# Induced attention with a gated feed-forward layer: loads and big transposes in turn, shared blocks moved, row sets a block earlier

## The chip, the cores and the metric

The kernel runs on one core of one Trainium2 chip. The metric is the device time of one execution in microseconds (us). Besides single times there is one profiled execution, which gives the start and the duration of every instruction, and for each DMA the time at which it landed.

## The reference

Input: `x` of 4 batches x 12416 tokens x 128 channels, 32 inducing rows of 128 channels, and the weights of a gated layer (gate and value 128 x 1536, out 1536 x 128). Cut to what matters:

```python
def mab(q, kv):                          # softmax attention, scale 1/sqrt(128)
    s = scale * (q @ kv.transpose(0, 2, 1))
    a = exp(s - s.max(-1)); a /= a.sum(-1) + 1e-9
    return a @ kv
h   = mab(I, x)                          # 32 rows look at all tokens of a batch
y   = mab(x, h)                          # every token looks at the 32 rows
out = (sigmoid(y @ w_gate) * (y @ w_val)) @ w_out
```

## The kernel before, in words

**Two stages per batch.** In the first stage the 32 inducing rows attend to all tokens of a batch and give `h` (32 x 128). In the second stage every token attends to the 32 rows of `h`. Since the softmax weights of a token are only 32 numbers, `h` is multiplied into the weights once per batch (`hw`, `hw_mm`), and the gated layer then reads the 32 weights of a token (`rep`) in place of its 128 channels.

**Blocks.** The second stage goes over 97 blocks of 512 tokens: 24 a batch (three row sets `d` of two quads `i` of four blocks `r`) and one mixed block of the tails. A block has 12 feature slices `j`. For every pair of slices TensorE makes the gate (`g`) and ScalarE the tanh (`T`, `g_tanh`, L482). For each of the four chunks of a block TensorE fills the value of two slices (`va`) and of one slice (`vb`), and VectorE multiplies both with `T` (`v_mul`, L495). TensorE then multiplies the products `u` with `w_out` into `acc` (L538). ScalarE copies `acc` out (`oT`), SyncE transposes it by DMA (`on`, L562) and GpSimd issues the store (L566).

**Shared blocks.** In the blocks that `SHARED` names (the number within the batch), the first chunk is not VectorE's. Two extra slots among the gate slots fill its value, ScalarE copies it from PSUM to SBUF (`v`, L833), and GpSimd makes the product in two operations a slice (`v_mul_pool`, L508 and L511): two slices for the first extra slot, one for the second. Such a block has three chunks on VectorE.

**Row sets.** For each row set of eight blocks, `rep_events` (L691) lays a chain: job `s2` on TensorE with the exponential on ScalarE; `e2_dma`, a transpose; `s2_sum`, five additions on GpSimd that halve each time; `s2_rec`, a reciprocal on VectorE; `a2_mul`, two multiplications on GpSimd; `a2_dma`, two transposes; `rep_put`, two writes to a DRAM buffer `dt`; `rep_get`, two times four reads from it into `rep`. All DMAs of the chain are SyncE's.

**The next batch's first stage** runs beside the second stage of this one. Six quads of 2048 tokens are loaded by GpSimd with a cast (`load_x`, L125), transposed by one big DMA each (`xT_dma`, L192), scored two quads at a time (job `s1`, then `a1_dma`, L217), and summed into `h` (job `h`, `h_mm` L243, with `h_add` on VectorE, L267). `hfin` and `hw` end the batch.

**What sets the order.** Every engine's instructions stand in the order of the program; there is no scheduler. The string `PLAN` (L23) has one word for each block: `A` and `B` are the chunk's two value fills with their products, `G` is the next gate slot (`W` the same in a padded form), `J` the next extra job, and a letter from `a` to `l` the output matmul of that slice. Gate slots run about one and two thirds blocks ahead, since ten `T` buffers exist. DMAs and GpSimd's steps are tied to places: `at(n, k, f)` puts `f` ahead of chunk `k` of block `n` (written n.k below), and `put(n, k, ...)` queues a job in that order, which the next `J` takes. A place says only after which instructions of its engine a step stands. An engine with nothing to wait for runs ahead of the place; one that waits holds up all that stands behind it in its own queue.

```python
for q, ((ln, lk), (hn, hk)) in enumerate(zip(loads, hs)):
    at(n0 + ln, lk, load_x, nb, q)
    at(n0 + ln + 1, 2, xT_dma, nb, q)
    put(n0 + hn, hk, "h", nb, q)
```

Of the kernel before, what the change touches and what calls it, by code (L numbers as in the profile page):

```python
# [10 lines left out]
F16 = mybir.dt.float16  # L11
# [11 lines left out]


PLAN = (
    "GAGBWGAabGBcGAfeGBdGAhBWgJ AGilkjBGGAabcBGAfGBedGAhGgBiG AlkjBGGAbacBGAfWBedGAhJBgG "
    "AilkjBGGAabcBGAfWBedGAhGgBiG AlkjBGGAbaBcWAGfeBGdAGBhGg AGilkBjGAJBabcAGefBGdAGhgBGi "
    "AGlBkjJAGBaGbAGcGBefGAdhGBgG AikljBGGAbBaefGAdGBchG AgGBikGAljBJAGaBGbcGAGfBedG "
    "AhGgBiGAlJBkGAjJBGAGbacBfeG AGdhBgiAGlkjBGGAbBJaAGcfBGe AGdhBGgAGiBkljGAGBabef "
    "AGdBJcGAhgBGikAGljJBGAGbaBcfG AGedBGgAGhBilGAGkjBJAGBaGbcG AefGBdGAhgGBiGAkljBJAGbaGBcf "  # L30
    "AGeGdBhGAgiWBlGAkjJBG AGabfBecGAGdBghGAikGBlJjAGBaGbcG AfGBedGAhJBgGAilkjBGGAabBcefG "
    "AdGBghGAilkjBGGAbaBGcGAfBJe AGdhBGgAGilBkjGAGBabef AGdcBGgGAhiBkljGAGBbacfAGedgGBhG "
    "AilkjBGGAbacBWAGfBedGAhGgBiG AlkjBGGAbacBJAGfBGeAGdghBG AGilBkjGAGBbafeAGdcGBG "
    "AghBGiAGklBJjAGGBbacfAGedBGg AGhiBGkAGljBJAGBGabcGAeGfBdG AgGhBiGAlGkBjGAJbaBcAGfeBGdh "
    "AGgiGBkGAljBJAGbGBGa AGBefdGAGchBgGAiGBlkjGAGBabce AGfBJdAGhgBWiAGkBljGAGBbacf "
    "AGedGBghAGilkjBGGAabBGcAGefBGd AGhgBGiAGlkjBJGABbGafG AedGBcGAhgBWiGAklBjJGAaGbBcG "
    "AfeGBdGAhJBgGAilkjBGGAbacBfe AGdgGBhGAilkjBGGAaBJbAGceBGf AGdhBGgAGilkBjGAGBabef "
    "AGdcGBgGAhiBGkAGljBJAGBGbaceG AGfBdghGAiWBklGAjJBGAGabcBfG AGedBhGAgGBGAGilkJjBGAaGbBGcf "
    "AGedBWhAGgilBkjGAJaBbG AceGBfGAdhBWgGAilBkjGAJbBaG AcfGBeGAdBWghAGilkBjGGAabBceG "
    "AfGdBgGAhiBGGAlkjBGGAbacGBe AGfdBhGAGgilBkjAGGBbafe AGcdBGhAGgiBlkjGAGBabceAGfdBgG "  # L40
    "AGhikBljGAGBabcGAefBGdAGhgBGi AGlBkjGAGaBbcGAJBfeGAdGBhgG AilkjBGGAabfBedGAcGBhgG "
    "AikljBJGAbGBacGAfWBedAGhgGBiG AlkGBGAjBJAGbBGacGAfGBedG AhGgBiGAlGkBjGAGBbacfAGeBJd "
    "AGghBGiAGlkjBJGABbaGfG AedBchGGAgiBkljGAGBabceGAfBdGgh AGikljBGAJBbaGAcWBfeGAdGhBgG "
    "AilkjBGAGabBcGAeGBGAGfdBGh AGgikBGAGlBjJAGBbGae AGfdBGhGAgciBGAGlkBjJGABbGacG "
    "AfGeBdGAhgWBiGAkljBJAGbacBfG AeGBdGAhJBgGAilkjBGGAbacBfGG AedBghiGAlkjBGGAbaBfedG "
    "AGhBgciAGlkBjJGAaBbGcfAGedWBhgG AiGlBkGAjJBGAGabBcWAGfBedG AGhgBiGAlGkBjJAGBbaGGcAGfBJe "
    "AGdBGhgGAilkBjGAGbBafeG AdcGBgGAhiGBkGAljBJGAbacBfG AeGBdhGAgGiBlGAkjBWGAabBcefG "
    "AdGBghGAilkjBGGAbacBfeGAGBdGh AGgilBkjGAGBefbaAGdgBWh AGicBkljGAGBbacGAefdBGAGghBiG "
    "AGlkjBGAGBbacGAfeBWdAGhgBGi AGlBkjGAGBabcGAefGBdGAhGBgiG AkljBGGAfeBbadGAhWBgcG "
    "AilkBjGGAabBcGAfeGBdGAhgBGiG AlkBjGGAbaBcAGfWBedGAhgGBiG AlkjBJAGbacBGAfGeBGAdWBhgG "  # L50
    "AikljBGGAfedBabGAGhBgiG AclkjBGGAabcBGAGfBedGAhWgBiG AGlkBjGAGBbacAGefBWAGdhgBG "
    "AGiBlkjGAGBabcAGefBdJAGGhBgG AikGlBjGAGBabfeAGdgBWh AGciBkljGAGBabcGAefBGdAGhgiBG "
    "AGkljBGAGBbacGAfeBWdGAhgBGi AGlBkjGAGBabcGAefGBdGAJBhgG AilkjBGGAfeBbadGAGhgBcG "
    "AilBkjGGAabBcGAfBGedGAhgWiBG AlkjBGGAbacBGAGfeBdGAGBhgiG AlkjBGGAabcBGAGfeBdGAGBGhg "
    "AGiBlkjGAGBefabAGdhBWgG AicBlkjGAGBbacGAefBGdAGhgBGi AGlkBjGAGBbacGAefBWdGAhgBGi "
    "AGlBkjGAGBbacGAefGBdGAhGgBiG AlkjBGGAfebBadGAgWBhcG AikBljGGAabBcGAfeGBdGAhGBgiG "
    "AlkBjGGAbBacAGfBWedAGhgBGiG AlkBjGAGbaBcGAefBGdGAhGgBiG AlkjBGGAbafBeGAdWBhgG "
    "AcikBljGABaGbAcfeBdAhgBilkj"
)
SHARED = (3, 7, 11, 15, 19, 23)  # L60


@with_exitstack
def kernel(
# [9 lines left out]
    nc = tc.nc  # L74
# [26 lines left out]
    smp = ctx.enter_context(tc.tile_pool(name="smp", bufs=2))  # L101
# [308 lines left out]
    NBK = len(blocks)  # L410
# [274 lines left out]
    def at(n, k, fn, *a):  # L685
        ev.setdefault((n, k), []).append(lambda: fn(*a))

    def put(n, k, *a):
        extra.append((n, k, a))

    def rep_events(n, b, d):  # L691
        put(n, 1, "s2", b, d)
        at(n + 1, 0, e2_dma, b, d)
        at(n + 1, 3, s2_sum, b, d)
        at(n + 2, 3, s2_rec, b, d)
        at(n + 2, 3, a2_mul, b, d, 0)
        at(n + 2, 3, a2_mul, b, d, 1)
        at(n + 3, 0, a2_dma, b, d, 0)
        at(n + 3, 1, a2_dma, b, d, 1)
        at(n + 3, 2, rep_put, b, d, 0)  # L700
        at(n + 3, 3, rep_put, b, d, 1)
        at(n + 4, 0, rep_get, b, d, 0)
        at(n + 4, 1, rep_get, b, d, 1)

    def m_mul():
        e2s["m", "a2"] = s2n_mul("m", 0, nc.gpsimd, B)
# [20 lines left out]
    assert ND == 3  # L727
    for b in range(B):
        n0 = b * BB
        rep_events(n0 + 2, b, 1)  # L730
        rep_events(n0 + 10, b, 2)
        nb = b + 1
        if nb < B:
            if b == 0:
                loads = ((1, 0), (2, 0), (5, 0), (6, 0), (8, 0), (9, 0))
                s1s, s1t, fin = (5, 9, 12), 6, 16
                hs = ((8, 1), (9, 1), (12, 2), (13, 1), (14, 3), (15, 1))
            else:
                loads = ((-10, 0), (-7, 0), (-4, 0), (-1, 0), (2, 0), (5, 0))
                s1s, s1t, fin = (-2, 5, 9), 0, 14  # L740
                hs = ((1, 1), (3, 1), (7, 1), (8, 1), (12, 1), (13, 1))
            for q, ((ln, lk), (hn, hk)) in enumerate(zip(loads, hs)):
                at(n0 + ln, lk, load_x, nb, q)
                at(n0 + ln + 1, 2, xT_dma, nb, q)
                put(n0 + hn, hk, "h", nb, q)
            at(n0 + loads[1][0], 1, load_tail, nb)
            at(n0 + loads[1][0] + 1, 3, xTt_dma, nb)
            for e, sn in enumerate(s1s):
                put(n0 + sn, 1, "s1", nb, [2 * e, 2 * e + 1])
                at(n0 + sn + 1, 1, a1_dma, nb, [2 * e, 2 * e + 1])  # L750
            put(n0 + s1t, 1, "s1t", nb)
            put(n0 + fin, 1, "hfin", nb)
            put(n0 + fin + 1, 1, "hw", nb)
            at(n0 + fin + 2, 1, hw_pad, nb)
            rep_events(n0 + fin + 2, nb, 0)
        else:
            put(n0 + 6, 1, "s2m")
            at(n0 + 7, 1, s2n_sum, "m", 0, B)
            at(n0 + 7, 1, m_mul)
            at(n0 + 8, 1, m_dma)  # L760
# [76 lines left out]
    def out_one(n, j):  # L837
        out_mm(n, j, us.pop((n, j)))
        if done_out[n] == NJ:
            out_store(n)  # L840
        if stores and (done_out[n] == 10 or n >= NBK - 2):
            stores.popleft()()

    words = PLAN.split()
# [63 lines left out]
```

The softmax here doesn't subtract the row's maximum and nothing guards it: scores larger than these inputs give would overflow.

## Time and profile before

| | us |
|---|---|
| median of 8 runs | 709.43 |
| lowest, highest | 704.78, 711.69 |
| the profiled execution: its time | 707.12 |
| its span, first to last instruction | 705.3 |
| VectorE / ScalarE / TensorE busy in it | 666.3 / 662.5 / 678.9 |
| GpSimd busy in it | 309.5 |

How to read it: the span is 1.8 us shorter than the execution's own time, which has the start and the end in it too. The profile's page gives the busy time of each engine, a row of tenths over 40 slices of the span, and the costliest groups of instructions with their mean duration in ns and the idle time ahead of them. PE is TensorE, DVE VectorE, ACT ScalarE, POOL GpSimd, SP SyncE; PEld are TensorE's weight loads. SyncE has no busy time: its lines (SPq) show how long the issue of a DMA stood in its queue. A group "u<-T,va" writes `u` from `T` and `va`; buffer numbers are left out. L is the line in the kernel. Until about 29 us the first batch's own first stage runs by itself; then block 0 begins. Block 96 ends at about 700 us.

### The profile page before, as it was taken

The numbers are of one execution on the slowest core, as the hardware profiler recorded it, in microseconds if no ns is written. First come the engines' busy times: TensorE is split into PE (matmuls) and PEld (weight loads), VectorE is DVE, ScalarE is ACT, GpSimd is POOL, SyncE is SP. The second block draws the span as 40 slices with busy tenths as digits, with TensorE's granted clock in tenths as the row PEclk, the third lists the DMA queues.
The fourth block names the chain that finished last, engine by engine and source line by source line (L and its number), as shares of the span: only waits on it lengthen the run. The fifth ranks groups of instructions, "written<-read, shape, count | busy, mean of one in ns | idle before, by whom it ended". The sixth has DMA issues, their size and how long they took to land.

```text
span 705.3 us, 13070 instructions
## 1 busy us (share of the span) xinstructions
PE 678.9 (96%) x4561; PEld 238.4 (34%) x4561; DVE 666.3 (94%) x792; ACT 662.5 (94%) x773; POOL 309.5 (44%) x389
## 2 busy tenths in 40 slices
PE   8899899999999999999999989999999999999997
PEld 5433233333333333333333323333333333333334
DVE  2599899999999999999999989999999999999997
ACT  4699899999999989999999989999999999999995
POOL 5234506426536334365353540744632633633523
PEclk9999999999999999999999999999999999999999
DMA  9687999875898673676786792354282353362223
GB/s 176 99 130 131 192 164 174 171 138 100 169 175 135 124 153 75 128 156 111 162 163 110 132 204 60 84 136 82 60 143 68 68 150 75 68 150 69 65 49 76
DMA packets 163955, 85.95 MB, mean 122 GB/s; under 512 B 133392, under 2 KB 148144, under 8 KB 163888
## 3 DMA queue, kind: packets, MB, share of 16 engines
q1 hardware_dynamic: 143904, 45.95, 36.6%
q0 software_dynamic: 19696, 39.03, 26.5%
q8 instruction: 35, 0.57, 0.3%
q14 instruction: 32, 0.26, 0.1%
q10 hardware_dynamic: 288, 0.13, 0.1%
HBM read 39.34 MB, written 28.31 MB: 96 GB/s over the span
## 4 chain that ended last, share of the span: by engine, by line
PE 69%; ACT 10%; DVE 9%; DMA 5%; issue 3%; POOL 2%; SPq 1%; DVEq 0%; ACTq 0%; POOLq 0%
PE acc L538 30%; PE g L428 16%; PE vb L428 9%; DVE u L495 9%; PE va L428 8%; ACT T L482 6%; DMA a2T<-a 2%; ACT v L833 1%; DMA a1n<-e 1%; PE warm L190 1%; ACT oT L560 1%; PE h L255 1%; PE s L324 1%; PE x L428 1%; DMA rep<-dt 1%
## 5 line engine op out<-in xcount | busy, mean ns | idle before, releaser
L482 ACT ACTIVATE T<-g 128x1024 f16<-128x1024 f32 x582 | 559.6, 1038 | 17.2 <-PE va L428 7.8
L495 DVE SCALAR_TENSOR_TENSOR u<-T,va 128x1024 f16<-128x1024 f16 x365 | 444.8, 1219 | 5.8 <-PE va L428 2.8
L538 PE MATMUL acc<-u,wo 128*128 128x512 f16 x1083 | 340.8, 383 | 0.6
L495 DVE SCALAR_TENSOR_TENSOR u<-T,vb 128x512 f16<-128x512 f16 x365 | 248.7, 681 | 2.3 <-PE vb L428 1.8
L428 PE MATMUL g<-rep,hw 32*128 32x512 f16 x1086 | 205.3, 384 | 4.2 <-DMA rep<-dt 1.7
L428 PEld LDWEIGHTS <-hw 32*128 32x128 f16 x1854 | 77.4, 91 | 221.0 <-issue 207.9
L428 PE MATMUL va<-rep,hw 32*128 32x512 f16 x722 | 141.2, 380 | 4.5 <-DVE u L495 2.3
L566 POOL DMA_DIRECT2D out_dram<-on x96 | 53.8, 561 | 204.4 <-DMA on<-oT 185.1
L538 PEld LDWEIGHTS <-wo 128*128 128x128 f16 x1152 | 93.9, 97 | 146.1 <-issue 92.1
L428 PE MATMUL vb<-rep,hwp 128*128 128x512 f16 x361 | 137.9, 382 | 1.5 <-DVE u L495 0.7
L508 POOL TENSOR_TENSOR vt<-v,T 128x512 f32<-128x512 f32 x69 | 79.8, 1156 | 116.6 <-ACT v L833 72.5
L511 POOL TENSOR_TENSOR x<-vt,v 128x512 f16<-128x512 f32 x69 | 87.4, 1266 | 5.4
L428 PEld LDWEIGHTS <-hwp 128*128 128x128 f16 x450 | 43.8, 97 | 58.5 <-issue 26.4
L560 ACT ACTIVATE oT<-acc 128x512 f16<-128x512 f32 x96 | 59.1, 615 | 2.4 <-PE acc L538 1.8
L833 ACT COPY v<-x 128x1024 f32<-128x1024 f32 (+1 forms) x46 | 37.9, 824 | 0.7 <-PE x L428 0.6
L370 POOL TENSOR_TENSOR a<-e2n,rc 128x512 f16<-128x512 f16 x22 | 22.5, 1039 | 21.8 <-DVE rc L361 21.7
L538 PE MATMUL acc<-x,wo 128*128 128x512 f16 x69 | 24.1, 387 | 0.9 <-POOL x L511 0.7
L428 PE MATMUL g<-rep,hwp 128*128 128x512 f16 x66 | 19.6, 379 | 0.6 <-ACT T L482 0.6
L353 POOL TENSOR_TENSOR tree<-tree 128x256 f32<-128x256 f32 (+2 forms) x33 | 16.1, 489 | 2.6
L353 POOL TENSOR_TENSOR tree<-e2n 128x512 f32<-128x512 f16 x11 | 12.6, 1149 | 10.4 <-DMA e2n<-e 10.2
L127 POOL DMA_DIRECT2D xq<-in_x_dram x23 | 13.0, 566 | 0.8 <-POOLq L892 0.8
L584 DVE COPY xT<-xt 128x1024 f16<-128x1024 f16 x6 | 4.2, 692 | 9.6 <-PE xt L579 9.6
(98 smaller groups left out, 211.6 us busy)
## 6 DMA issues: line engine op xcount, KB each, us to landing
out_dram<-on POOLq DMA_DIRECT2D x96, 256.0 KB, 3.0
xq<-in_x_dram POOLq DMA_DIRECT2D x23, 512.0 KB, 6.9
rep<-dt SPq DMA_DIRECT2D x88, 128.0 KB, 2.9
dt<-a2T SPq DMA_DIRECT2D x22, 128.0 KB, 2.3
on<-oT SPq DMA_TRANSPOSE x96, 2.5
xq<-in_x_dram POOLq DMA_DIRECT2D x2, 256.0 KB, 14.5
wg<-in_moe_w_gate_dram POOLq DMA_DIRECT2D x1, 384.0 KB, 15.9
wv<-in_moe_w_val_dram POOLq DMA_DIRECT2D x1, 384.0 KB, 16.7
```

Source lines behind the costliest of these rows:

```text
L127: nc.gpsimd.dma_start(t[:], x[b, ds(q * QT, QT)].rearrange("(p j) c -> p (j c)", j=QT // P))
L353: nc.gpsimd.tensor_tensor(out=nxt, in0=cur[:, :, 0:w], in1=cur[:, :, w:2 * w], op=ALU.add)
L370: nc.gpsimd.tensor_tensor(out=a2[:], in0=e2n[:, i], in1=rc[:, i].unsqueeze(3).to_broadcast((P, 4, 4, M)), op=ALU.mult,)
L428: nc.tensor.matmul(ps[:, ds(col, TOK)], weights(k["b"]), rep[rows, 4 * k["i"] + k["r"]], start=True, stop=True,)
L482: nc.scalar.activation(out=Ts[(bi, p)][:, :, 0:T], in_=ps[:].rearrange("p (a t) -> p a t", a=2)[:, :, 0:T], func=AF.Tanh, scale=0.5,)
L495: nc.vector.scalar_tensor_tensor(out=u[:, :, 0:T], in0=Ts[(bi, j0 // 2)][:, j0 % 2:j0 % 2 + n, 0:T], scalar=1.0, in1=ps[:].rearrange("p (a ...
L508: nc.gpsimd.tensor_tensor(out=t[:], in0=v, in1=Ts[(bi, j0 // 2)][:, j0 % 2 + jj, :], op=ALU.mult)
L511: nc.gpsimd.tensor_tensor(out=u[:, jj, :], in0=t[:], in1=v, op=ALU.add)
L538: nc.tensor.matmul(accs[bi][:, 0:T], wo16[:, j, :], u, start=(c == 0), stop=(c == NJ - 1))
L560: nc.scalar.activation(out=oT[:], in_=accs[bi][:], func=AF.Copy, scale=0.5)
L566: nc.gpsimd.dma_start(out[ds(row0, QT)].rearrange("(p j) c -> p j c", j=QT // P)[:, 4 * k["r"]:4 * k["r"] + 4, :], on[:],)
L833: nc.scalar.copy(out=v32[:], in_=ps[:, 0:p * TOK])
```

## The change

It moves work and adds one kind of instruction; what is computed stays.

1. *First batch's loads.* The six quads of batch 1 are loaded every two blocks, at 0.2, 2.2, 4.2, 6.2, 8.2 and 10.2 (before: 1.0, 2.0, 5.0, 6.0, 8.0, 9.0), and each big transpose is placed four chunks after its load (before six; the later batches keep six).
2. *Fence.* Ahead of every load but a batch's first, GpSimd copies two elements a row out of the previous quad's transposed tile. So it waits for that transpose to land before it issues the load.
3. *Shared blocks* are those numbered 1, 5, 9, 13, 17, 21 in place of 3, 7, 11, 15, 19, 23. There are 23 in both kernels.
4. *Row sets* begin one block earlier within a batch (and the first set of batch 1 too), the sum stands a quarter of a block later after its start, the reciprocal and the multiplications three quarters of a block later; the two transposes, the two writes and the two groups of reads stand together at one place each.
5. *h jobs and scores* of the next batch are placed anew; in the later batches the third and fourth h stand at 8.1 and 8.3 in place of 7.1 and 8.1. In batch 0 the finish is one block earlier.
6. *Stores.* A block's store is issued when the block after the next has four of its output matmuls, in place of when the next block has ten.
7. `PLAN` is new for all this (its words are left out here). It has the same number of each letter except that five gate slots lose the padded form.

```diff
-SHARED = (3, 7, 11, 15, 19, 23)
+SHARED = (1, 5, 9, 13, 17, 21)
...
+    def load_fence(b, q):
+        t = smp.tile([P, 2], F16, tag="fence", name=f"fence_{b}_{q}")
+        nc.gpsimd.tensor_copy(out=t[:], in_=xTs[b][:, ds(q * QT, 2)])
...
     def rep_events(n, b, d):
         put(n, 1, "s2", b, d)
         at(n + 1, 0, e2_dma, b, d)
-        at(n + 1, 3, s2_sum, b, d)
-        at(n + 2, 3, s2_rec, b, d)
-        at(n + 2, 3, a2_mul, b, d, 0)
-        at(n + 2, 3, a2_mul, b, d, 1)
-        at(n + 3, 0, a2_dma, b, d, 0)
-        at(n + 3, 1, a2_dma, b, d, 1)
-        at(n + 3, 2, rep_put, b, d, 0)
-        at(n + 3, 3, rep_put, b, d, 1)
-        at(n + 4, 0, rep_get, b, d, 0)
-        at(n + 4, 1, rep_get, b, d, 1)
+        at(n + 2, 0, s2_sum, b, d)
+        at(n + 3, 2, s2_rec, b, d)
+        for i in range(2):
+            at(n + 3, 2, a2_mul, b, d, i)
+            at(n + 3, 3, a2_dma, b, d, i)
+            at(n + 4, 1, rep_put, b, d, i)
+            at(n + 4, 3, rep_get, b, d, i)
...
-        rep_events(n0 + 2, b, 1)
-        rep_events(n0 + 10, b, 2)
+        rep_events(n0 + 1, b, 1)
+        rep_events(n0 + 9, b, 2)
...
-                loads = ((1, 0), (2, 0), (5, 0), (6, 0), (8, 0), (9, 0))
-                s1s, s1t, fin = (5, 9, 12), 6, 16
-                hs = ((8, 1), (9, 1), (12, 2), (13, 1), (14, 3), (15, 1))
+                loads = ((0, 2), (2, 2), (4, 2), (6, 2), (8, 2), (10, 2))
+                s1s, s1t, fin = ((5, 0), (9, 2), (12, 3)), 6, 15
+                hs = ((8, 1), (8, 3), (13, 0), (13, 2), (14, 2), (15, 0))
+                wait = 4
             else:
                 loads = ((-10, 0), (-7, 0), (-4, 0), (-1, 0), (2, 0), (5, 0))
-                s1s, s1t, fin = (-2, 5, 9), 0, 14
-                hs = ((1, 1), (3, 1), (7, 1), (8, 1), (12, 1), (13, 1))
+                s1s, s1t, fin = ((-2, 1), (5, 1), (9, 1)), 0, 14
+                hs = ((1, 1), (3, 1), (8, 1), (8, 3), (12, 1), (13, 1))
+                wait = 6
             for q, ((ln, lk), (hn, hk)) in enumerate(zip(loads, hs)):
+                if q:
+                    at(n0 + ln, lk, load_fence, nb, q - 1)
                 at(n0 + ln, lk, load_x, nb, q)
-                at(n0 + ln + 1, 2, xT_dma, nb, q)
+                at(n0 + ln + (lk + wait) // 4, (lk + wait) % 4, xT_dma, nb, q)
                 put(n0 + hn, hk, "h", nb, q)
             at(n0 + loads[1][0], 1, load_tail, nb)
-            at(n0 + loads[1][0] + 1, 3, xTt_dma, nb)
-            for e, sn in enumerate(s1s):
-                put(n0 + sn, 1, "s1", nb, [2 * e, 2 * e + 1])
-                at(n0 + sn + 1, 1, a1_dma, nb, [2 * e, 2 * e + 1])
+            at(n0 + loads[1][0] + 2, 1, xTt_dma, nb)
+            for e, (sn, sk) in enumerate(s1s):
+                put(n0 + sn, sk, "s1", nb, [2 * e, 2 * e + 1])
+                at(n0 + sn + 1, 0, a1_dma, nb, [2 * e, 2 * e + 1])
...
-        if stores and (done_out[n] == 10 or n >= NBK - 2):
+        while stores and (n >= NBK - 2 or len(stores) > 1 and done_out[n] == 4):
             stores.popleft()()
```

## The prediction

> **What bounds the kernel now.** I read the page's first part, then the busy time of every engine by stretches, then the queues of SyncE (SP) and GpSimd (POOL) around the stretches that fall short. The first part names three engines as full:
>
> ```profile
> PE 678.9 (96%) x4561; PEld 238.4 (34%) x4561; DVE 666.3 (94%) x792; ACT 662.5 (94%) x773; POOL 309.5 (44%) x389
> L495 DVE SCALAR_TENSOR_TENSOR u<-T,va 128x1024 f16<-128x1024 f16 x365 | 444.8, 1219 | 5.8 <-PE va L428 2.8
> L495 DVE SCALAR_TENSOR_TENSOR u<-T,vb 128x512 f16<-128x512 f16 x365 | 248.7, 681 | 2.3 <-PE vb L428 1.8
> ```
>
> The two VectorE products of one chunk start 1.77 us apart from the next pair (they overlap by some 65 ns a piece), so an ordinary block of four chunks takes 7.05 us and a shared block of three 5.31 us. Read from the starts of the products, most blocks take just that, plus 0.41 for each h sum and 0.33 for each reciprocal. VectorE is the metronome; TensorE and ScalarE have a little air. The stretches show where the metronome stops (after a stretch's length come the busy times of PE, PEld, DVE, ACT and POOL):
>
> ```profile
> core 0: us, PE busy (x) PEld busy (x) DVE busy (x) ACT busy (x) POOL busy (x), PEclk, DMA share, GB/s
> 75.00:108.00 33.00, 30.19 (x202) 9.93 (x201) 28.97 (x35) 28.30 (x34) 10.82 (x13) 0.95 1.14 173
> 108.00:225.00 117.00, 115.97 (x772) 38.97 (x770) 116.53 (x139) 115.77 (x136) 59.64 (x73) 1.00 0.85 150
> 225.00:257.00 32.00, 30.05 (x206) 10.02 (x204) 30.02 (x37) 30.00 (x36) 15.80 (x20) 1.00 0.85 162
> 257.00:400.00 143.00, 140.83 (x913) 47.78 (x910) 142.31 (x169) 140.92 (x165) 66.07 (x83) 1.00 0.65 128
> 400.00:425.00 25.00, 22.14 (x138) 6.90 (x136) 21.10 (x26) 21.30 (x26) 11.20 (x13) 0.93 0.84 164
> 425.00:700.00 275.00, 270.47 (x1683) 94.91 (x1682) 274.38 (x320) 267.34 (x310) 117.06 (x136) 1.00 0.40 89
> ```
>
> Idle VectorE: 4.03 us in 75:108, 1.98 in 225:257, 3.90 in 400:425, together 9.9; in the other 535 us shown 1.8. So the most that any reordering can win is near 12 us, and 9.9 of it sits in three places. The first place, by the queue of SyncE and then VectorE:
>
> ```profile
> 66.62 1.20 SPq L384 DMA_TRANSPOSE a2T<-a  x1
> 69.20 2.20 SPq L562 DMA_TRANSPOSE on<-oT  x1
> 71.49 1.22 SPq L384 DMA_TRANSPOSE a2T<-a  x1
> 72.81 7.02 SPq L390 DMA_DIRECT2D dt<-a2T  x2
> 79.92 1.82 SPq L397 DMA_DIRECT2D rep<-dt  x4
> ...
> 83.81 1.22 DVE L495 SCALAR_TENSOR_TENSOR u<-T,va 128x1024 f16<-128x1024 f16 x1 [2.39 <-PE va L428]
> 85.98 0.69 DVE L495 SCALAR_TENSOR_TENSOR u<-T,vb 128x512 f16<-128x512 f16 x1 [0.94 <-PE vb L428]
> ```
>
> Two loads went out at 67.56 and 68.67. The second a2T was issued at 71.49 and landed at 79.49; the second dt, which reads it, stood at the head of SP's queue until then (7.02 us for two), and the rep reads behind it came late for block 8's first gate matmul. The other two places are one story: a row set's a2T transposes meet a load, SP stands, and behind them the a1n transpose is late for an h matmul:
>
> ```profile
> 414.62 2.01 SPq L397 DMA_DIRECT2D rep<-dt  x4
> 416.67 1.23 SPq L221 DMA_TRANSPOSE a1n<-e  x1
> ...
> 420.36 0.61 PE L245 MATMUL h<-a1n,ones 128*128 128x128 f16 x4 [2.64 <-DMA a1n<-e]
> ...
> 421.56 0.42 DVE L271 TENSOR_TENSOR hacc<-hacc,h 128x256 f32<-128x256 f32 x1 [2.95 <-PE h L255]
> ```
>
> **What the Trainium skill says.** "DMA: Bandwidth & Descriptors", section "Issuing engines are not separate DMA queues": DMAs of all engines share the same 16 DMA engines and interleave. The trace agrees that they share, but it is harsher than interleaving: over the 18 loads after 38 us, DMAs issued inside a load landed mostly 0.2 to 4 us after that load's own end, however small; a2T issued 0.9 us or more ahead of a load took 2.4 to 3.8 us, 0.3 to 0.7 us ahead 4.7 to 7.4. "TensorE: Matmul & The Clock Gate", section "What's actually happening": an idle PE falls to half clock and needs a few us of work to return. The trace agrees: after the two long waits matmuls show 0.61 instead of 0.39 us, and the granted clock is 0.93 to 0.95. "GPSIMD Engine Reference", "1. Specifications": GpSimd shares SBUF interfaces with VectorE, in contention for VectorE instructions with two SBUF inputs. The product reads one input from PSUM, and it took 1.16 to 1.22 us throughout, GpSimd busy or not: moving GpSimd work costs VectorE nothing.
>
> **The change part by part.** The totals of VectorE, ScalarE and TensorE work stay (23 shared blocks, 49 extra jobs, 365 pairs); five gate pairs lose the padded form. So only waits change. Positions (block.chunk) are turned into time with 1.765 us a chunk.
>
> *h a block later (8.1 and 8.3 for 7.1 and 8.1), row sets a block earlier.* From a1n's issue at 6.0 to h there are now over two blocks (15 us) for one (7 us). SP stood 4 to 7 us in the bad cases, so both waits for a1n go: -1.98 and -3.90. Likewise the old wait in 75:108 goes as it was, -4.03. Removed: 9.9.
>
> *What is late next, first batch.* The reciprocal and both a2_mul are at 4.2, 63.5 us. But the instruction order on GpSimd puts the first pair of shared block 5 ahead of a2_mul. Its gate slot is in chunk 4.0 (59.9); such v copies started 0.2 to 1.5 us after their chunk and take 1.03, so 62.2; 2 x (1.15 + 1.27) and gaps make 5.1: 67.3. A store 0.6, two a2_mul 2.1: 70.0. The fence and load q2 follow at 70.1; the second a2T leaves SP at 69.0 + 1.2 = 70.2, level with the load, so it lands near the load's end, 77. Then on SP: dt 0.4, an output transpose 1.2, and, which is new, the big transpose xT of q2 before the rep reads (1.3 to 3.2 us with no load in flight, 2.4 taken): 81.0; the first half of rep lands 2.7 later, 83.7. VectorE runs out at 38.4 + 6.98 + 14.1 + 7.38 + 5.31 + 7.05 + 1.77 = 81.0 (block 5 is the short one now) and restarts 1.2 after rep, as before: idle 3.9, and 1.1 of slow matmuls after it (1.64 before). Taken 5.0; bounds 2.0 (load and xT at their shortest) and 7.5 (both at the long end).
>
> *Batch 1, rows of blocks 8 to 15.* Same order: a2_mul ends 7.4 us after chunk 28.2, the load leaves at 10.7, so the a2T are free of it, but the rep reads (from 11) fall inside it and land near 17.5 to 18.5. The gate matmul that needs them comes at about 17.1. Taken 1.0 (0 to 2). The rows for blocks 40 on meet the next batch's first load in the same way: 1.0 (0 to 2).
>
> *Batch 2, rows of blocks 56 on.* Both pairs of block 53 stand ahead of a2_mul: it ends 8.5 us after chunk 52.2, the load leaves at 9.3, the second a2T 0.6 before it: lands at 13.5, the dt inside the load at 16.2, rep at 18.9, wanted at 16.8. Idle 2.1 and slow clock 0.9: taken 3.0 (0.5 to 4.5).
>
> *First batch, end.* a2_mul behind the pair of block 13, rep for block 16 due at 15.1 within 1 us of its landing, h of q4 at 14.2 within 1.5 us of a1n: 0.7 (0 to 3). In the other row sets without loads the chain from reciprocal to rep is 15 us against 17 to 23 available: 0.3.
>
> *Fence, stores, two jobs in shared blocks.* 15 fences, two elements each; the nearest row, a 32x128 copy, takes 0.29: 4 us of GpSimd in all, hidden in its 56% idle time, if the xT has landed; I find it landed 3 us or more before in every batch after the first. If that cover goes, the load and the stores behind it slip, and nothing due within 3 us. Stores go out half a block later, when their transpose (2.4 to 9.9 us) has landed: GpSimd's 185 us of waiting for it shrinks, worth nothing off the path. Six shared blocks carry two jobs; VectorE has 5.3 us there and TensorE nearly as much: 0.5 (0 to 2).
>
> Sum: -9.9 + 5.0 + 1.0 + 1.0 + 3.0 + 0.7 + 0.3 + 0.5 = +1.6. The profiled execution took 707.1 (span 705.3), so 708.7; the median of the eight runs is 709.4, 2.3 above it, so 711.0.
>
> **Rivals.** (a) The queues do clear: v copies come early in their slots, xT takes 1.8, loads 6.0. Then the first batch returns 2.5, batch 2 only 0.5, the rest 1. Net -5.9: 703.5. For it: the long waits of before came from two loads issued 1.1 us apart, and this pairing is gone. Against: a2_mul demonstrably moves behind 5 us of other GpSimd work. (b) Slower, by one mechanism: GpSimd's line. Each us that a shared pair ends later moves a2_mul, a2T and then the load onto each other; where a2T falls behind the load, rep slips by the whole load, some 4 us more than I took, once in each of batches 0, 1 and 2 (and the idle PE then runs slow): returns 20 in place of 11.5, net +9.5, 719. It decides when a v copy is over 1 us later than taken. (c) The products of shared blocks come late for their output matmuls (0.7 us waited in all before): pairs have 7 to 12 us from slot to use, as before, so 0 to 2 us; within the likeliest case.
>
> **How the numbers follow.** Likeliest, stalls change place: 0.45, 707.5 to 714.5. (a) 0.24. (b) 0.29. 0.02 for worse. Under 705.9 (-0.5%, about what a measurement of this kernel can tell from no change) lies most of (a): faster 0.22; over 713.0 lies (b) and the top of the likeliest: slower 0.36; the rest 0.42. The range takes in (a) and most of (b): 703.5 to 719.
>
> **What would show it.** Right: a VectorE gap near block 7 or 8 for the va that waits for rep, with a2T, xT and rep stacked on SP; a gap near block 55; none for h at blocks 31 and 55; a2_mul starting right after an x product, not after the reciprocal. Wrong: no gap over 1 us after 75 us (then the chain from copy to rep is shorter than I made it), or gaps for x, xT or the reciprocals (then fence or sums stand in the way, which I took as covered).

## The result and the profile after

| | before | changed |
|---|---|---|
| median, us | 708.39 (32 runs) | 721.6 (11 runs) |
| lowest, highest | 703.03, 714.02 | 718.18, 723.63 |
| the profiled execution: its time, span | 707.12, 705.3 | 723.2, 721.4 |
| VectorE idle from 29.5 us to its last instruction | 12.9 | 27.0 |

The ratio is 1.019, with a 95% interval of 1.016 to 1.022: slower by 13 us, where 1.6 was forecast. Medians here and below are of all runs; ratios leave out runs more than 1.5% above the fastest of the same kernel. First the totals and the two product groups of the changed kernel's page:

```profile
PE 681.8 (95%) x4561; PEld 236.5 (33%) x4561; DVE 668.3 (93%) x792; ACT 662.8 (92%) x773; POOL 311.0 (43%) x404
...
L500 DVE SCALAR_TENSOR_TENSOR u<-T,va 128x1024 f16<-128x1024 f16 x365 | 444.9, 1219 | 21.1 <-issue 9.3
...
L500 DVE SCALAR_TENSOR_TENSOR u<-T,vb 128x512 f16<-128x512 f16 x365 | 248.8, 682 | 4.0 <-PE vb L433 3.5
```

The products take what they took (1219 and 682 ns), so VectorE itself is not slower. The idle time ahead of the `va` products went from 5.8 to 21.1 us. The stretches say where (PE, PEld, DVE, ACT and POOL busy; clock, DMA share and GB/s at the end):

```profile
core 0: us, PE busy (x) PEld busy (x) DVE busy (x) ACT busy (x) POOL busy (x), PEclk, DMA share, GB/s
75.00:110.00 35.00, 30.15 (x205) 9.27 (x205) 29.41 (x35) 28.33 (x34) 10.79 (x14) 0.95 0.97 176
110.00:200.00 90.00, 85.45 (x571) 28.43 (x568) 86.16 (x104) 85.41 (x100) 43.13 (x59) 1.00 0.78 135
200.00:212.00 12.00, 9.35 (x44) 2.74 (x44) 7.83 (x10) 7.96 (x10) 0.92 (x3) 0.86 1.11 210
212.00:425.00 213.00, 209.15 (x1354) 69.89 (x1351) 211.12 (x249) 210.38 (x246) 101.61 (x129) 1.00 0.70 128
425.00:440.00 15.00, 7.94 (x35) 2.13 (x35) 5.28 (x6) 5.16 (x7) 0.53 (x1) 0.66 0.89 203
440.00:710.00 270.00, 266.40 (x1621) 90.44 (x1617) 269.28 (x315) 265.09 (x308) 117.57 (x137) 1.00 0.42 90
```

VectorE is idle for 5.6 us in 75:110 (block 7), 3.8 in 110:200 (mostly blocks 14 to 16), 4.2 in 200:212 (block 23) and 9.7 in 425:440 (block 55). Such idle time at a block is called a stop below. The one at 55 is the largest. GpSimd's queue, then SyncE's (an SPq line is the time that the issue stood, with its count), then VectorE's:

```profile
411.04 1.15 POOL L513 TENSOR_TENSOR vt<-v,T 128x512 f32<-128x512 f32 x1
412.27 1.26 POOL L516 TENSOR_TENSOR x<-vt,v 128x512 f16<-128x512 f32 x1
413.50 2.05 POOL L375 TENSOR_TENSOR a<-e2n,rc 128x512 f16<-128x512 f16 x2
415.49 0.59 POOL L571 DMA_DIRECT2D out_dram<-on  x1
416.08 0.20 POOL L138 COPY fence<-xT 128x2 f16<-128x2 f16 x1
416.21 0.53 POOL L127 DMA_DIRECT2D xq<-in_x_dram  x1
416.73 0.53 POOL L571 DMA_DIRECT2D out_dram<-on  x1
...
414.57 3.42 SPq L389 DMA_TRANSPOSE a2T<-a  x2
418.64 9.33 SPq L395 DMA_DIRECT2D dt<-a2T  x2
428.08 1.19 SPq L567 DMA_TRANSPOSE on<-oT  x1
429.38 3.91 SPq L402 DMA_DIRECT2D rep<-dt  x8
...
433.27 1.22 DVE L500 SCALAR_TENSOR_TENSOR u<-T,va 128x1024 f16<-128x1024 f16 x1 [8.61 <-issue]
435.02 0.69 DVE L500 SCALAR_TENSOR_TENSOR u<-T,vb 128x512 f16<-128x512 f16 x1 [0.53 <-PE vb L433]
436.52 1.22 DVE L500 SCALAR_TENSOR_TENSOR u<-T,va 128x1024 f16<-128x1024 f16 x1 [0.81 <-ACT oT L565]
```

Here a2_mul (`a<-e2n,rc`) starts at 413.50, as the last product of shared block 53 ends. It did not wait for the reciprocal, which was made 6.6 us earlier. The second a2T (one of the row set's two transposes, `a2_dma`) leaves at 415.86 and the load at 416.21. The second `dt`, which needs that a2T, stands at the head of SyncE until 427.64 (that is the 9.33), and the reads of `rep` follow at 429.38. VectorE stood for 8.6 us for the block that needs them, and 1.3 more. How long the two a2T took from issue to landing:

```profile
DMA to landing us min/median/max: 4.1/7.9/11.8
```

At block 7 it is the same order, with a2_mul right behind a product and a store and the second a2T (71.1) beside a load (70.9):

```profile
68.74 2.06 POOL L375 TENSOR_TENSOR a<-e2n,rc 128x512 f16<-128x512 f16 x2
...
85.69 1.22 DVE L500 SCALAR_TENSOR_TENSOR u<-T,va 128x1024 f16<-128x1024 f16 x1 [4.38 <-PE va L433]
```

At block 23 the same chain is late, and the load falls into its last part:

```profile
188.17 1.26 POOL L516 TENSOR_TENSOR x<-vt,v 128x512 f16<-128x512 f32 x1
189.38 0.59 POOL L571 DMA_DIRECT2D out_dram<-on  x1
189.99 2.06 POOL L375 TENSOR_TENSOR a<-e2n,rc 128x512 f16<-128x512 f16 x2
...
202.37 0.18 POOL L138 COPY fence<-xT 128x2 f16<-128x2 f16 x1 [2.17 <-DMA xT<-xq]
202.61 0.53 POOL L127 DMA_DIRECT2D xq<-in_x_dram  x1
...
197.99 1.79 SPq L198 DMA_TRANSPOSE xT<-xq  x1
199.89 4.80 SPq L402 DMA_DIRECT2D rep<-dt  x8
...
205.87 0.69 DVE L500 SCALAR_TENSOR_TENSOR u<-T,vb 128x512 f16<-128x512 f16 x1 [2.74 <-PE vb L433]
207.75 1.22 DVE L500 SCALAR_TENSOR_TENSOR u<-T,va 128x1024 f16<-128x1024 f16 x1 [1.19 <-PE g L433]
```

a2_mul again follows a shared product (190.0, behind the pair of block 21). The big transpose goes ahead of the eight reads, and when it lands (202.3) it releases the load through the fence, in the midst of them: the first three reads land 3.3 to 4.5 us after issue, the last five 6.2 to 8.1.

Of the eleven row sets of the changed kernel, a2_mul starts right behind a shared product (or the store after it) in nine. Only four of these stop VectorE, so where the chain has time to spare the late a2_mul costs nothing.

### The profile page after: what moved, and what is told of

Read it like the earlier page. It is cut to its first block, busy times and chain, and to the rows that moved or that the text cites. A ratio compares the mean times of both kernels' runs of the same rounds, so it can differ in the third digit from the quotient of the medians.

```text
span 721.4 us, 13070 instructions
## 1 busy us (share of the span) xinstructions
PE 681.8 (95%) x4561; PEld 236.5 (33%) x4561; DVE 668.3 (93%) x792; ACT 662.8 (92%) x773; POOL 311.0 (43%) x404
## 4 chain that ended last, share of the span: by engine, by line
PE 64%; ACT 11%; DVE 10%; DMA 6%; issue 5%; POOL 1%; SPq 1%; DVEq 0%; ACTq 0%; POOLq 0%
PE acc L543 28%; PE g L433 16%; DVE u L500 10%; PE vb L433 9%; ACT T L487 8%; PE va L433 7%; DMA rep<-dt 2%; DMA xq<-in_x_dram 2%; DMA a2T<-a 2%; ACT v L839 1%; ACT oT L565 1%; PE s L329 1%; PE x L433 1%; DMA a1n<-e 1%; PE h L260 1%
## 5 line engine op out<-in xcount | busy, mean ns | idle before, releaser
L500 DVE SCALAR_TENSOR_TENSOR u<-T,va 128x1024 f16<-128x1024 f16 x365 | 444.9, 1219 | 21.1 <-issue 9.3
L433 PE MATMUL g<-rep,hw 32*128 32x512 f16 x1096 | 209.5, 386 | 17.3 <-DMA rep<-dt 14.7
L543 PE MATMUL acc<-x,wo 128*128 128x512 f16 x69 | 23.7, 381 | 0.2
L358 POOL TENSOR_TENSOR tree<-e2n 128x512 f32<-128x512 f16 x11 | 12.7, 1150 | 18.5 <-DMA e2n<-e 18.4
L433 PE MATMUL g<-rep,hwp 128*128 128x512 f16 x56 | 16.6, 379 | 2.2 <-DMA rep<-dt 1.5
L127 POOL DMA_DIRECT2D xq<-in_x_dram x23 | 12.9, 564 | 1.5 <-POOLq L898 0.8
L589 DVE COPY xT<-xt 128x1024 f16<-128x1024 f16 x6 | 4.1, 691 | 10.1 <-PE xt L584 10.1
```

The lines of the kernel that those rows point to most:

```text
L127: nc.gpsimd.dma_start(t[:], x[b, ds(q * QT, QT)].rearrange("(p j) c -> p (j c)", j=QT // P))
L358: nc.gpsimd.tensor_tensor(out=nxt, in0=cur[:, :, 0:w], in1=cur[:, :, w:2 * w], op=ALU.add)
L433: nc.tensor.matmul(ps[:, ds(col, TOK)], weights(k["b"]), rep[rows, 4 * k["i"] + k["r"]], start=True, stop=True,)
L500: nc.vector.scalar_tensor_tensor(out=u[:, :, 0:T], in0=Ts[(bi, j0 // 2)][:, j0 % 2:j0 % 2 + n, 0:T], scalar=1.0, in1=ps[:].rearrange("p (a ...
L543: nc.tensor.matmul(accs[bi][:, 0:T], wo16[:, j, :], u, start=(c == 0), stop=(c == NJ - 1))
```

## The experiments

**Theory A**, formed from this: what costs the time is the late start of a2_mul on GpSimd. With the reciprocal three quarters of a block later after the row set's start, the products of a shared block (1.15 + 1.27 us a slice and gaps: 5 us for two slices, 7.6 us for the three of block 53) stand ahead of it. The row set's chain then ends late, and beside a load, which stretches it. **Rivals**: B, the fence costs by holding GpSimd; C, the new place of the shared blocks costs in itself; D, output stores beside the load; E, the places of the row set's DMAs on SyncE; F, the fence is what pays; G, the late spacing is too late whatever GpSimd does.

Idle VectorE in the traces, us, summed over the blocks named ("all" is from 29.5 us to VectorE's last instruction; each row is one trace; the interval is that of the ratio to the kernel before, on the same chip):

| kernel | median | ratio, 95% | 7-8 | 14-16 | 23 | 31-33 | 55-56 | elsewhere | all |
|---|---|---|---|---|---|---|---|---|---|
| before | 708.4 | | 3.3 | 0.1 | 0.0 | 1.5 | 3.8 | 4.2 | 12.9 |
| changed | 721.6 | 1.016-1.022 | 5.5 | 3.1 | 4.2 | 0.5 | 10.1 | 3.6 | 27.0 |
| no fence | 727.3 | 1.024-1.041 | 9.3 | 2.5 | 8.5 | 2.2 | 6.9 | 3.2 | 32.6 |
| old spacing | 701.7 | 0.993-0.998 | 0.1 | 0.3 | 0.1 | 0.3 | 0.0 | 5.2 | 6.0 |
| load later | 715.4 | 1.010-1.022 | 5.7 | 2.6 | 6.2 | 0.3 | 2.6 | 3.8 | 21.2 |
| multiplications first | 709.3 | 1.003-1.008 | 0.1 | 0.3 | 0.1 | 0.3 | 0.2 | 14.0 | 15.0 |
| multiplications early, DMAs late | 704.0 | 0.996-1.000 | 0.1 | 0.3 | 0.1 | 0.3 | 0.8 | 6.3 | 7.9 |
| old spacing, no fence | 705.1 | 0.994-1.000 | 4.3 | 0.3 | 0.1 | 0.3 | 0.0 | 5.7 | 10.7 |
| old stores | 720.9 | 1.008-1.027 | 6.1 | 0.7 | 2.9 | 1.3 | 10.8 | 3.4 | 25.2 |
| reads first | 719.8 | 1.012-1.025 | 1.9 | 2.1 | 4.4 | 0.4 | 10.4 | 4.4 | 23.6 |
| pairs of block 53 held | 713.9 | 1.003-1.019 | 5.5 | 2.5 | 4.1 | 1.9 | 0.2 | 4.1 | 18.3 |

**No fence.**

```diff
-                if q:
-                    at(n0 + ln, lk, load_fence, nb, q - 1)
```

> The changed kernel without its 15 fences, all else the same. Theory A (row-set chains run into loads, whoever releases them): the load behind block 53 leaves 0.2 us earlier and still beside the second a2T, so the stop of 10.0 us at block 55 stays (8 to 11); the load in block 23 leaves at about 200 in place of 202.6, still ahead of or among the rep reads, stop there 3 to 6; in the first batch a second load leaves near 75 while a2T, dt and rep of block 8 are under way, stop there 5 to 9 in place of 5.2. Time 720 to 727. Rival B (the fence itself costs, by holding GpSimd 22.5 us for the transposes): the stops at 23 and 55 shrink to under 2 each, time 708 to 714.

Measured 727.3, a hair over A's range, and far from B's. The stops at 7 and 23 nearly double, since a load leaves earlier and deeper among the transposes and reads; the one at 55 stays, smaller (6.9, under the 8 expected). B falls: the 22.5 us that GpSimd stands at the fences do not cost time on balance, and what they keep apart is worth 5.6 us of idle time.

**Old spacing.** The row sets still begin a block earlier; only the distances within them go back.

```diff
-        at(n + 2, 0, s2_sum, b, d)
-        at(n + 3, 2, s2_rec, b, d)
+        at(n + 1, 3, s2_sum, b, d)
+        at(n + 2, 3, s2_rec, b, d)
-        for i in range(2):
-            at(n + 3, 2, a2_mul, b, d, i)
-            at(n + 3, 3, a2_dma, b, d, i)
-            at(n + 4, 1, rep_put, b, d, i)
-            at(n + 4, 3, rep_get, b, d, i)
+        at(n + 2, 3, a2_mul, b, d, 0)
...
+        at(n + 3, 0, a2_dma, b, d, 0)
...
+        at(n + 3, 2, rep_put, b, d, 0)
...
+        at(n + 4, 0, rep_get, b, d, 0)
...
```

> The changed kernel with the row sets' steps at the old distances from their start (sums, reciprocal, multiplications, transposes, writes and reads half a block to three quarters earlier, transposes at two places); all else as changed. Theory A: a2_mul is then ahead of the shared pair of block 5 and of both pairs of block 53 on GpSimd, the a2T leave 4 to 7 us before the load; the stop at block 55 falls from 10.0 to under 3, that at block 7 from 5.2 to under 3, that at block 23 changes too since the rep reads come earlier: time 707 to 713. Rival C (the reciprocal later is harmless, the shared blocks' place in itself costs): no change beyond 2 us, 719 to 723. A further possibility: VectorE waits for sums at the reciprocal, 1 to 3 us in places, which takes some of it back.

Measured 701.7: below A's range, so A's sign was right and its size too small, and 0.5% faster than the kernel before (interval 0.993 to 0.998). All stops of the table are gone, and the trace shows no wait of VectorE for the sums, which I had thought possible. C falls: the shared blocks are still at their new places. GpSimd, then SyncE, at the place of the 10 us stop:

```profile
388.07 2.05 POOL L375 TENSOR_TENSOR a<-e2n,rc 128x512 f16<-128x512 f16 x2 [2.08 <-DVE rc L366]
390.07 0.59 POOL L571 DMA_DIRECT2D out_dram<-on  x1
392.21 1.14 POOL L513 TENSOR_TENSOR vt<-v,T 128x512 f32<-128x512 f32 x1 [1.54 <-ACT v L842]
...
400.51 0.53 POOL L127 DMA_DIRECT2D xq<-in_x_dram  x1
...
389.14 2.52 SPq L389 DMA_TRANSPOSE a2T<-a  x2
391.76 0.52 SPq L395 DMA_DIRECT2D dt<-a2T  x1
395.48 1.19 SPq L567 DMA_TRANSPOSE on<-oT  x1
396.76 0.53 SPq L395 DMA_DIRECT2D dt<-a2T  x1
397.40 4.02 SPq L402 DMA_DIRECT2D rep<-dt  x8
```

Now a2_mul waits for the reciprocal (the releaser is `rc`) and the pair comes after it. Both a2T leave 10 us or more before the load, and all reads but the last are out when it does.

**Load later.** The sixth quad's load two blocks later in batches 1 and 2.

```diff
-                loads = ((-10, 0), (-7, 0), (-4, 0), (-1, 0), (2, 0), (5, 0))
+                loads = ((-10, 0), (-7, 0), (-4, 0), (-1, 0), (2, 0), (7, 0))
```

> The changed kernel with one load moved in each of batches 1 and 2: the sixth quad of the next batch (and its fence and big transpose) two blocks later, 31.0 for 29.0 and 55.0 for 53.0, so behind the row set's chain. Theory A: the stop at block 55 (10.0 us of idle VectorE) goes to under 2, the others stay (5.2, 3.3, 4.1 within 1.5): time 711 to 715. Rival D (the stop at 55 comes from the two output stores issued beside it, or from GpSimd being late, and not from the load): the second a2T still takes over 8 us and the stop stays over 7: 718 to 722.

Measured 715.4, at the edge of A's range; the stop at 55 fell from 10.1 to 2.6, where A had under 2. With no load in flight the second a2T landed after 5.3 us, beside two stores, and `dt` and `rep` followed. So of the 10 us the load makes 7.5, and the late a2_mul alone 2.6.

**Multiplications first.** The late spacing stays; the pairs of blocks 5, 13 and 21 of each batch wait until a2_mul has been placed.

```diff
+    hold = {n for n in shared if n % BB in (5, 13, 21)}
+    for n in sorted(hold):
+        at(n - 1, 2, hold.discard, n)
...
             n, w, v32 = h
+            if n in hold:
+                continue
```

> The changed kernel, in which the GpSimd products of the shared blocks 5, 13 and 21 of each batch are held until the row set's multiplications have been placed; so on GpSimd a2_mul goes ahead of the pairs, with the spacing of the row sets as changed. Theory A with GpSimd's order as the cause: at 53 a2_mul runs near 408 in place of 413.5, both a2T land before the load leaves at 416, only the rep reads meet it: stop 0 to 3 in place of 10.0; at block 7 a2T leave near 65 to 66, land 68.5 and dt and rep leave before the load: stop under 2 in place of 5.2; block 23 about as before. Time 708 to 713. If GpSimd's order is not what matters (rival C): 719 to 723. Cost of the edit: the pairs end 2 to 3 us later, their slices wait at TensorE 0 to 1 us in a few blocks.

Measured 709.3, in A's range: the stops of the changed kernel are gone (7-8, 14-16, 23 and 55-56 together 0.7 us, from 22.9), that at 23 too, which I had expected to stay. My cost for the edit was too small: new stops came at blocks 5 (3.7), 21 (1.2), 76 to 78 (3.2) and 85 (1.9), at each of which the output matmul waits for a held product. TensorE at block 5:

```profile
72.50 1.01 PE L543 MATMUL acc<-x,wo 128*128 128x512 f16 x2 [2.75 <-POOL x L516]
```

The value fills stand behind this matmul. A pair can't be late in every block; at 53 and 13 it could.

**Pairs of block 53 held.** The same edit for one block (shown against "multiplications first").

```diff
-    hold = {n for n in shared if n % BB in (5, 13, 21)}
+    hold = {53}
```

> The changed kernel with the GpSimd products of one shared block only, block 53, held until the multiplications of the row set for blocks 56 on have been placed. Theory A: a2_mul runs some 5 us earlier there, the stop of 10.0 us at block 55 goes (under 1), no other changes: 709 to 713. If the collision of the second a2T with the load alone made that stop, holding the pairs (the load still leaves at its place) keeps 5 us or more of it: 715 to 719.

```profile
407.97 2.05 POOL L375 TENSOR_TENSOR a<-e2n,rc 128x512 f16<-128x512 f16 x2 [7.35 <-DVE rc L366]
...
418.29 0.53 POOL L127 DMA_DIRECT2D xq<-in_x_dram  x1
```

Measured 713.9, just over A's range; the stop at 55 went from 10.1 to 0.2 with the load at its place in the program and all else the same. The new 1.9 at 31 to 33 is not the edit's (block 53 comes later); it shows by how much a stop can differ between two executions. Both a2T landed after 2.5 us, 3 us and more before the load left (418.3); the load then fell among the reads, seven of which landed 7 to 8 us after issue, and the chain had the time for it. So the two together make the stop: without the load 2.6 is left, without the delay 0.2.

**Multiplications early, DMAs late.** As "old spacing" for sums, reciprocal and a2_mul; the DMAs of the row set stay at their changed places.

```diff
-        at(n + 2, 0, s2_sum, b, d)
-        at(n + 3, 2, s2_rec, b, d)
+        at(n + 1, 3, s2_sum, b, d)
+        at(n + 2, 3, s2_rec, b, d)
         for i in range(2):
-            at(n + 3, 2, a2_mul, b, d, i)
+            at(n + 2, 3, a2_mul, b, d, i)
```

> The changed kernel with only GpSimd's and VectorE's part of a row set at the old distances (sums, reciprocal, multiplications); the DMAs of the row set stay at the changed places on SyncE (transposes together, writes together, reads together, behind the big transpose of the third quad in the first batch). Theory A with GpSimd's order as the cause: a2_mul is ahead of the pairs, a2T leave before the loads, the stops at 14/15, 23 and 55 go to under 1 each; in the first batch the reads of rep still stand behind a big transpose that waits for its load, so 0 to 2.5 us stay at block 7: 702 to 706. If the places on SyncE matter as much (rival E): half or more of the 18 us stays, 710 to 716.

Measured 704.0, as A said; E falls. The interval overlaps that of "old spacing", so no difference between the two is shown.

**Old spacing, no fence.** The edits of the first two kernels together.

> The kernel with the old spacing (e2_old_spacing) and without the fences. Theory A: with the row sets' chains ahead of the loads there is nothing left for the fence to protect except the chain of two loads close together in the first batch; stops stay under 2 in all: 700 to 705. If the fence is what pays in e2_old_spacing (rival F): the two loads near 68 and 74 meet rep reads or a1n again, 3 to 6 us of stops in the first batch: 705 to 709.

Measured 705.1, at the edge; the two intervals overlap, so the times do not separate it from "old spacing". The traces do: 4.3 us idle at 7 to 8 against 0.1, within the 3 to 6 that F gave. A second load went out 3.6 us after the first, a big transpose stood 10.3 us on SyncE, and a1n behind it was late for h (2.8). I had expected under 2: the fence is worth 4 to 5 us even with early chains. So F holds in part: of the 6.9 us by which "old spacing" idles less than the kernel before, 4.7 go with the fence. It does not explain the loss: taking the late spacing away saves 21 us of idle time with the fence (27.0 to 6.0) and 22 without it (32.6 to 10.7).

**Old stores.**

```diff
-        while stores and (n >= NBK - 2 or len(stores) > 1 and done_out[n] == 4):
+        if stores and (done_out[n] == 10 or n >= NBK - 2):
```

> The changed kernel with the old rule for output stores (one as soon as the next block has ten of its output matmuls). Theory A: the stops stay, the stores only add some bytes beside the loads; 717 to 723. Rival D' (two stores beside the load make the second a2T 4 us later): the stop at 55 falls from 10.0 to 5 or 6 and the time to 712 to 716; or, with GpSimd standing at a store for its transpose ahead of a2_mul, it grows to 724 or more.

Measured 720.9, as A said: in time the store rule is worth nothing that can be seen here. In the trace the stop at 14 to 16 is 0.7 in place of 3.1 and others are longer. It does not decide D, for two stores still left within 1 us of the load at 53.

**Stores away.** To settle D, the stores of two blocks were to leave only after the load of 53 had landed.

```diff
-        while stores and (n >= NBK - 2 or len(stores) > 1 and done_out[n] == 4):
+        while stores and n not in (52, 53) and (
+                n >= NBK - 2 or len(stores) > 1 and done_out[n] == 4):
```

> The changed kernel with no output stores near the load of block 53: those of two blocks are issued one to two blocks later, all others as changed. The load then leaves about 0.2 us ahead of the second a2T. If the stores stretch them: the load takes 6 to 7 us and the a2T lands at its end (6 to 7.5 us after issue), the stop at block 55 falls from 10.1 to 4 to 6, time 714 to 718. If they do not: load and a2T take 9.5 us or more as before, stop 9 to 11, time 719 to 723.

Measured 721.5 (ratio 1.016 to 1.025), stop 7.9: neither. The edit missed: both stores left right behind the load (416.2 and 416.8) in place of one ahead and one behind. The load took 7.2 us and the second a2T 8.9. What stretches the load to 10.3 in the changed kernel stays open. The two stores do not do it by themselves: in the second and third kernel of "the other order" below a store 0.7 us ahead, one 0.5 us behind and a second a2T all stand at this load too, and it took 6.6 and 6.7. What can be seen is that DMA nearly stood for a while. The changed kernel, 414 to 434 in 40 slices of 0.5 us, tenths of DMA engine time and GB/s:

```profile
DMA  0004899979001009393069969910074906899999
GB/s 0 0 0 90 170 302 306 275 29 28 0 9 9 0 9 33 26 82 35 20 143 246 229 139 361 320 57 0 12 250 83 178 1 184 293 260 201 346 346 268
```

and the kernel without fences at its own place of that stop, 423 to 443:

```profile
DMA  0059999907797999500000729058969999999999
GB/s 0 0 108 188 279 303 234 50 21 137 126 231 133 229 275 361 169 8 16 21 20 8 262 57 199 6 174 252 307 168 322 371 316 229 227 213 196 119 233 285
```

In the first, 6 us (418 to 424) pass at 0 to 82 GB/s with a load, two stores, an a2T and a `dt` all on their way; in the second, with almost the same issues, there are dips of 1 us and, near the load's end, of 2.5 us, and the load took 8.5. "Old stores" and "reads first" show the standstill too.

**Reads first.** The big transpose of the first batch's third quad behind the reads of `rep`, which are laid at 5.3 before it.

```diff
-                at(n0 + ln + (lk + wait) // 4, (lk + wait) % 4, xT_dma, nb, q)
+                if (b, q) == (0, 2):
+                    at(5, 3, xT_dma, nb, q)
+                else:
+                    at(n0 + ln + (lk + wait) // 4, (lk + wait) % 4, xT_dma, nb, q)
```

> The changed kernel with the big transpose of the first batch's third quad placed half a block later on SyncE, behind the reads of rep for block 8 and not ahead of them. The step of the forecast that it tests: the big transpose ahead of the reads costs 2.4 us there. If right, the reads leave near 79.1 in place of 81.2, and the stop at block 7 falls from 5.2 to 2.5 to 3.5; the rest as in the changed kernel: 716 to 720. If the stop stays at 5, the second dt write and not the big transpose sets it.

Measured 719.8. The stop at block 7 went from 5.5 to 1.9: the transpose ahead of the reads had cost 3.6 us, more than the 2.4 of the forecast. The time does not resolve the 3.6; the trace does.

**The other order: old shared blocks with the late spacing.** Three kernels have the shared blocks and the `PLAN` of the kernel before, with row sets a block earlier in the late spacing; for that, extra jobs (`J`) were moved within the words. The first is the changed kernel with this exchange, and all 49 jobs are placed by hand. The second and third are the kernel before with the row sets' lines, the fences and the stores of the change and 8 jobs moved; the second has the changed first-batch loads too, and the third has neither these loads nor fences in the first batch.

```diff
-SHARED = (1, 5, 9, 13, 17, 21)
+SHARED = (3, 7, 11, 15, 19, 23)
...
```

> The changed kernel with the shared blocks where they were (3, 7, 11, 15, 19, 23) and the order of chunks, gate slots and output matmuls of the kernel before, the extra jobs moved to the changed places; late row sets, fences, loads, h jobs and stores as changed. Theory A as an interaction: the late reciprocal hurts only because a shared pair stands in front of a2_mul; here the pairs of block 7 come after it, a2_mul runs within 2 us of the reciprocal, a2T leave 4 us or more before the load: the stops at 7, 23 and 55 fall to 0 to 2 each, 703 to 709. Rival G (the late spacing in itself is too late for rep, whatever GpSimd does): stops of 3 to 8 us stay at 7 and 55, 713 to 722.

> The kernel before, with its shared blocks and its order of chunks and gate slots, in which only the row sets begin a block earlier with the late spacing (eight extra jobs moved by one block for it), and the first batch's loads, the fences and the stores are as changed; h jobs and scores stay as before. On GpSimd a2_mul then comes straight after the reciprocal and the load straight after a2_mul. Theory A, in the form that the runs so far leave: the second a2T is hit by the load (6 to 11 us) all the same, but a2_mul is 5 to 7 us earlier against the due time of rep, and that covers it: no stop over 1.5 us for rep at blocks 7, 23 and 55; the stops for h at 31 and 55 as before (2 to 4 each) or longer; 704 to 713. Rival G (the late spacing in itself is too late): stops of 4 us or more for rep at 7 and 55, 715 to 724.

> As e11_old_shared_late, but with the first batch's loads as in the kernel before too (two together, no fence there), because the changed loads came too late for the score job of block 12. What is left of the change against the kernel before: row sets a block earlier with the late spacing, fences in the later batches, the stores. Theory A (late spacing hurts only behind a shared pair): a2_mul within 2 us of the reciprocal, no stop for rep over 2 us at 7, 23 and 55, none for a score at 12; stops for h of the kernel before (2 and 4 us) may stay: 705 to 713. Rival G (the late spacing in itself is too late for rep): stops of 4 us or more at 7 or 55 for rep, 715 to 722.

Measured 729.1, 724.1 and 717.0 (ratios 1.025 to 1.039, 1.018 to 1.031, 1.010 to 1.019): all outside A's ranges, and in time no support for it; the third lies in the range of G. In the traces the stops of 4 us or more for `rep` that G asked for are not there, as A says (7-8: 0.1, 2.2, 0.0; 23: 0.0 in all; 55-56: 0.4, 0.1, 0.0), even though the second a2T took 7 to 11 us beside the load in each. But other stops came: 27 us in small ones in the first, 7.8 at block 12 for a score in the second (the new loads are too late for the old score jobs), and in the third 8.2 at 31 to 33, where a1n (the transpose that the h matmuls read) stands behind the late reads and h waits 4.2, and 15 elsewhere. To tell the moved jobs from the late spacing, the third with the old spacing:

> As e12_old_shared_late_b (old shared blocks, row sets a block earlier, eight extra jobs moved for it, fences in later batches, changed stores), but with the old spacing of the row sets. Theory A: the moved jobs cost what is left in e12, so the small stops (11.7 us outside the named places) stay at 9 to 12; only the wait for h at 31 (8.2 in blocks 31 to 33) changes, to 1 to 3 with the reads of rep out of the way earlier: 709 to 713. Rival G: the late spacing is dear everywhere, so the small stops also fall to the 4 to 5 of the other kernels: 703 to 707.

Measured 740.2 (1.040 to 1.054). Both expectations miss, and the reason is worth more than either. A waits view of VectorE (us in all, times, longest), then GpSimd and VectorE at the longest:

```profile
DVE rc L352 <- POOL rs L344: 24.2, 8, 6.5
```

```profile
576.34 1.17 POOL L499 TENSOR_TENSOR vt<-v,T 128x512 f32<-128x512 f32 x1
577.58 1.26 POOL L502 TENSOR_TENSOR x<-vt,v 128x512 f16<-128x512 f32 x1
578.80 1.14 POOL L344 TENSOR_TENSOR tree<-e2n 128x512 f32<-128x512 f16 x1
580.02 1.62 POOL L344 TENSOR_TENSOR tree<-tree 128x256 f32<-128x256 f32 x3
581.72 0.24 POOL L344 TENSOR_TENSOR rs<-tree 128x32 f32<-128x32 f32 x1
...
581.99 0.35 DVE L352 RECIPROCAL rc<-rs 128x32 f32<-128x32 f32 x1 [6.48 <-POOL rs L344]
```

With the old shared blocks the pairs stand ahead of the sums, and a reciprocal at the old distance stops VectorE itself, eight times. In "old spacing" and in the third kernel above VectorE has no such wait. There the late spacing is a gain: 717.0 against 740.2. So the change holds two cures for one ill. Moving the shared blocks takes the pairs away from the sums, and moving the reciprocal waits for sums that are behind a pair. Either takes that wait away; with the first in place, the second only carries a2_mul behind the next pair. That the late spacing needs a pair in front of a2_mul to hurt is shown at the three places (7, 23, 55); that it is free otherwise is not (h at 31).

## Why the prediction was wrong

The mechanism was named, the signs it gave are there (gaps at 7 and 55 for `rep`, none for h at 31 and 55, a2_mul right after an x product), and the order of the queues was right; two terms of the sum were not.

- *Removed, -9.9.* The three stops of before are gone. But 9.9 was all the idle time of the windows, small gaps with it: by blocks the three come to 8.6, and in "old spacing", where nothing comes in their place, all idle time falls by 6.9.
- *First batch, +5.0.* 5.5, and as written: a2_mul right after an x product at 68.7 (forecast 67.9), second a2T at 71.1 (70.2), big transpose at 79.2, first `rep` landed at 84.4 (83.7).
- *Batch 1 (+1.0) and the rows for blocks 40 on (+1.0).* 0.5 and about 0.3: reads that meet a load land late, and still in time.
- *Batch 2, +3.0.* **The first step that failed: 10.1.** The forecast had a2_mul end 8.5 us after chunk 52.2 and the load leave at 9.3; they did so at 8.7 and 9.4. The mis-sized term is the landing of the second a2T: 4.8 taken from a start 0.6 us ahead of the load, 11.8 measured from a start 0.35 ahead (7.6 to 12.7 in the kernels with such a meeting at 53). Over all traces an a2T 0.4 to 0.7 us ahead of a load took 4.7 to 5.1 us and one 0.1 to 0.4 ahead 6.8 to 12.7, so 0.35 in place of 0.6 was enough to move the term; the load itself took 10.3 us, against 6.3 in the kernel before. In a chain that is serial on SyncE each of these 7 us reached VectorE.
- *"In the other row sets without loads", +0.3.* **The second: 4.2 at block 23.** That set was taken to have no load. It has one, at 23.0. The fence held it for 2.2 us and released it just then, where the forecast had every transpose landed 3 us before its fence; and the 15 us from reciprocal to `rep` left out the pair of block 21 (5.6 us, with a store) and the big transpose in front of the reads (1.8).
- *End of the first batch, +0.7.* 3.1, at the upper bound: the same order, behind the pair of block 13. With that pair held 0.3 is left; but "old stores" has 0.7 with the pair in front, so the pair is not all of it.
- *Fence and stores, +0.5.* Nothing lost; the fence gains 5 to 6 of idle time here, 4 to 5 with the old spacing.

The measured returns make 5.5 + 0.5 + 0.3 + 10.1 + 3.1 + 4.2 = 23.7 against 11.5 forecast. With the 9.9 removed that is a net 13.8, and idle time grew by 14.1. VectorE was busy 2.0 us more, though its instructions took the same sum, so they overlap less; together this is the 16.1 us between the two spans.

Rival (b) had the cause (a shared pair ahead of a2_mul, twice a stop of 4 to 7 us more than taken) and was near in time, 719 (its own figures, 20 returned and 9.9 removed, make 10.1 and not 9.5, so 719.5). But its point of decision was not: at block 53 no `v` copy had to be over 1 us later than taken, since a2_mul ended 0.2 us from the forecast. The order on GpSimd was enough, so that its number came so near is in part luck.

## What to carry to other kernels

Ask of every step moved later which long instruction of the same queue it falls behind, and keep the short step that starts a chain of DMAs ahead of the long one that nobody waits for soon. When two remedies for one collision go in together, build each alone: here the change without the second was 0.5% faster than before, and with both 1.9% slower. For this kernel, price an a2T that leaves within 0.4 us of a load at the load's end, not at its own length.

## What the hardware showed that was not expected

A second a2T issued within 0.4 us of a load, ahead of it or behind, took 6.3 to 12.7 us in all traces and landed between 0.2 us before and 3.4 us after the load, against 2.4 to 5.5 us with no load on its way. A start up to 0.4 us ahead bought nothing; one over 2 us ahead took 2.4 to 4.0. The load of block 53 (in "load later" of 55) in its turn took 9.8 to 11.2 us in four kernels and 6.3 to 8.9 in the twelve others, and in each of the four DMA moved less than 85 GB/s for 4 to 6.5 us of it (with one half microsecond of 122 between in one of them). The Trainium skill, "DMA: Bandwidth & Descriptors", section "Issuing engines are not separate DMA queues", says that DMAs of all engines interleave on the shared DMA engines; these runs show the sharing, and for a small one next to a large one a wait of about the large one's length. What makes the standstill is open.
